# Rounds taken in pairs, and a convolution moved into the weight fold: one change to a fused convolution and feed-forward kernel

## The chip, the core and the metric

The kernel runs on one core of a Trainium2 chip. A core has five engines that run side by side, each with its own queue of instructions in program order: TensorE (PE, matrix products), VectorE (DVE), ScalarE (ACT), GpSimd (POOL) and SyncE (SP). SP and POOL also issue the transfers between the chip's DRAM and the core's SBUF memory. Results of TensorE go to a small memory called PSUM, from which VectorE or ScalarE must copy them away before the place can be used again. The engines meet only at semaphores. The metric is the device time of one launch in microseconds (us), lower is better.

## What is computed

The reference has two stages. First a causal convolution over the sequence (8 sequences of 3904 positions, 192 channels): the channels form 8 heads of 24, each head has 7 taps, and the taps go through a softmax. Then a multiplicative feed-forward layer on all 31232 tokens.

```
w   = softmax(weight, axis=-1)                       # 8 heads x 7 taps
out[b, s, h, g] = sum_k w[h, k] * x_pad[b, s + k, h, g]   # 6 zeros ahead of each sequence
x2  = out.reshape(31232, 192)
a   = x2 @ w1                                        # 192 -> 1024
b   = x2 @ w2                                        # 192 -> 1024
y   = ((a * b) @ w3) @ w_out                         # 1024 -> 1024 -> 192
```

## The kernel before, in words

**Folding.** w3 and w_out are multiplied once (`W_sb` = w3 @ w_out, 1024x192), so that each token needs only two products. The *first product* makes `pa` = x2 @ w1 and `pb` = x2 @ w2, which ScalarE copies (`asb`, L376) and VectorE multiplies (`abT`, L377). The *second product* takes `abT` through `W_sb` (L388), and ScalarE copies the result (`osb`, L393), which SP stores to the output. The *fold of w3* is eight steps: TensorE transposes a row block of w3 (`w3_transpose`, L419), VectorE copies it (`w3T`, L422), TensorE multiplies it with w_out (`w3_product`, L428), ScalarE copies the result into `W_sb` (L430).

**Tiling.** The tokens are split into two streams (`NS` = 2, the first and the last four sequences), held in partitions 0 to 63 and 64 to 127. A *round* R is 512 tokens of each stream. There are 31 rounds, and the last one is half as wide. In a round the first product has eight steps `ft`, each of six matmuls into `pa` and six into `pb`. The second product of a round is two calls, one per stream, of 32 matmuls each.

**The convolution.** It is done on TensorE too. Windows of 64 positions (58 new ones and 6 of overlap) are multiplied with a banded matrix of one head's taps. There are 272 windows per stream, taken in ten *blocks* (`SIZES`). `conv(b, h0, nh)` convolves `nh` heads of block b: four matmuls per head (two halves of the block, two streams), one tile of PSUM (`cps`, L255), and a cast to `convo` (L272) by VectorE or ScalarE. A cast of a head whose 24 channels cross a multiple of 64 is split in two.

**From the convolution to the first product.** Blocks 0 to 2 (10 windows each) are transposed on TensorE (`pe_transposes`, L307) and copied to `xT` (L314). Later blocks are written by SP to a DRAM buffer (`store`, L292 and L298) and read back with transposing transfers (`transposes`, L335) into `xT`, a ring of four rounds.

**PSUM.** There is one pool of four tiles (`banks`, `bufs=4`), each of two banks, for everything: `pa`, `pb`, `ops`, `cps`, the transposes and the fold. They are handed out in turn, so a new tile waits until the tile four places earlier has been copied away.

**Order.** The order of all queues is that of the Python calls (`manual_schedule`). After a start-up (loading, the banded matrices, block 0), the first products of rounds 0, 1 and 2 run with the convolutions of blocks 1, 2 and 3 set between their steps (the `between` argument, L461 and after). Then come the fold, and a loop over R. Each pass of the loop has the first product of R (from R = 3 on), the second product of R - 2, two or three heads of the convolution as `plan` says, a `store` when a block is complete, and the transposing loads that have become possible. `load_x` for a later block is issued on POOL after a small copy (`pace`, L520) that waits for the end of a first product.

Of the kernel before, what the change touches and what calls it, by code (L numbers as in the profile page):

```python
# [17 lines left out]
def kernel(  # L18
# [10 lines left out]
    nc = tc.nc  # L29

    B, S, D = x.shape
    H, K = weight.shape
# [7 lines left out]
    NS = 2  # L40
    TS = B * S // NS
    CH = 512
    NR = -(-TS // CH)
    RING = 4 * CH
    LAG = 2
    Q = 64
    ST = Q - PAD
    NP = D // Q
    WB = -(-S // ST)
    NWIN = (B // NS) * WB  # L50
    LAST = S - (WB - 1) * ST
    SIZES = [10, 10, 10, 30, 32] + [36] * 5
    assert sum(SIZES) == NWIN
    NB = len(SIZES)
    FIRST = [sum(SIZES[:b]) for b in range(NB)]
# [3 lines left out]
    def tok(i):  # L59
        return (i // WB) * S + (i % WB) * ST  # L60
# [11 lines left out]
    def banks_bf16(name):  # L72
        return psum.tile([128, 16, 128], BF16, tag="banks", name=name)
# [18 lines left out]
    def load_x(b, parts=(0, 1)):  # L92
        tiles = xb_of.setdefault(b, [])
        zeros_of = zero_rows.setdefault(b, [])
        for i0, n in [v for e, v in enumerate(halves_of(b)) if e in parts]:
            xb = work.tile([128, n, D], BF16, tag="xb", bufs=6, name="xb")
            w = 0
            if i0 == 0:
                nc.vector.memset(xb[:, 0, :], 0.0)
                for r in range(NS):  # L100
                    nc.gpsimd.dma_start(out=xb[Q * r:Q * r + Q, 1:n, :], in_=x_spans(r, 1, n - 1))  # L101
                w = n
            while w < n:
                i = i0 + w
                m = min(n - w, WB - i % WB)
                at_end = i + m == NWIN
                if at_end:
                    m -= 1
                if m:
                    for r in range(NS):  # L110
                        nc.gpsimd.dma_start(out=xb[Q * r:Q * r + Q, w:w + m, :],  # L111
                                            in_=x_spans(r, i, m))
                if i % WB == 0:
                    zeros_of += [(xb, 0, w), (xb, 1, w)]
                w += m
                if at_end:
                    nc.gpsimd.memset(xb[Q:128, w, :], 0.0)
                    t = tok(NWIN - 1) - PAD
                    nc.gpsimd.dma_start(out=xb[0:Q, w, :], in_=x_rows[t:t + Q, :])
                    nc.gpsimd.dma_start(out=xb[Q:Q + PAD + LAST, w, :],  # L120
                                        in_=x_rows[TS + t:TS + t + PAD + LAST, :])
                    w += 1
            if len(halves_of(b)) == 1:
                tiles += [(xb, 0), (xb, SIZES[b] // 2)]
            else:
                tiles.append((xb, 0))
# [171 lines left out]
                    nc.sync.dma_start(out=dst[s0:s1], in_=src[s0:s1])  # L298
                w += m

    def pe_transposes(b):
        n = SIZES[b] // 2
        convo = convo_of[b]
        tps = banks_bf16("tps")
        for k in range(NP):
            for w in range(n):
                nc.tensor.transpose(  # L307
                    out=tps[:, k * n + w, :],
                    in_=convo[:, w, k].rearrange("p r g -> p (r g)"), identity=ident)
        t0 = tok(FIRST[b])  # L310
        for k in range(NP):
            dst = xT[k][:, t0:t0 + 2 * n * ST].rearrange("p (c w s) -> p c w s", c=2, w=n)
            src = tps[:, k * n:(k + 1) * n, :].rearrange("p w (c s) -> p c w s", c=2)
            (nc.scalar.copy if k == 1 else nc.vector.tensor_copy)(out=dst, in_=src[:, :, :, 0:ST])  # L314

    def pe_transpose(b, k, lead=0):
        n = SIZES[b] // 2
        convo = convo_of[b]
        tps = banks_bf16("tps")
        for w in range(lead):  # L320
            nc.tensor.transpose(out=tps[:, w % 2, :], in_=zeros[:, 0:128], identity=ident)
        for w in range(n):
            nc.tensor.transpose(
                out=tps[:, w, :],
                in_=convo[:, w, k].rearrange("p r g -> p (r g)"), identity=ident)
        t0 = tok(FIRST[b])
        dst = xT[k][:, t0:t0 + 2 * n * ST].rearrange("p (c w s) -> p c w s", c=2, w=n)
        src = tps[:, 0:n, :].rearrange("p w (c s) -> p c w s", c=2)
        return dst, src[:, :, :, 0:ST]

    def transposes(R, first=0):
        t0, t1 = max(R * CH, first), min((R + 1) * CH, TS)
# [21 lines left out]

    def first_product(R, between=None, lead=0):
        N = width(R)
        ab = work.tile([128, JT, NS, CH], BF16, tag="abT", bufs=LAG + 1, name="abT")
        abT_of[R] = ab
        r0 = (R * CH) % RING
        for ft in range(JT):  # L360
            pq = []
            for i in range(2):
                p = banks("pa" if i == 0 else "pb")
                pq.append(p)
                if ft == 0 and i == 0:
                    warm(lead, p)
                for k in range(NP):
                    for r in range(NS):
                        rs = slice(Q * r, Q * r + Q)
                        nc.tensor.matmul(  # L370
                            p[:, r, 0:N], w_of(i, k, r)[rs, ft * 128:(ft + 1) * 128],
                            xT[k][rs, r0:r0 + N],
                            start=(k == 0), stop=(k == NP - 1))
            pa, pb = pq
            asb = work.tile([128, NS, CH], BF16, tag="asb", bufs=3, name="asb")
            nc.scalar.copy(out=asb[:, :, 0:N], in_=pa[:, :, 0:N])  # L376
            nc.vector.tensor_tensor(out=ab[:, ft, :, 0:N], in0=asb[:, :, 0:N],  # L377
                                    in1=pb[:, :, 0:N], op=ALU.mult)
            if between and ft in between:
                between[ft]()  # L380
# [30 lines left out]
    def load_w3(jt):  # L411
        w3b_of[jt] = stage.tile([128, DFF], BF16, tag="w3b", bufs=JT, name="w3b")
        nc.gpsimd.dma_start(out=w3b_of[jt], in_=w3r[:, jt, :])
# [47 lines left out]
    swap_w(1, 0, (V, A))  # L461
    for k in (0, 2, 1):
        swap_w(k, 1, (P, P if k == 1 else V))
    load_x(3)
    load_wo()
    for jt in range(JT):
        load_w3(jt)
    load_x(4)
    load_x(5)

    def seq(*fs):
        def run():
            for f, *a in fs:
                f(*a)
        return run

    first_product(0, lead=2, between={
        3: seq((conv, 1, 0, 4)),
        5: seq((conv, 1, 4, 4)),
        7: seq((pe_transposes, 1), (conv, 2, 0, 4))})  # L480
    first_product(1, {
        0: seq((conv, 2, 4, 4)),
        2: seq((pe_transposes, 2), (store, 2, 26)),
        7: seq((conv, 3, 0, 1), (conv, 3, 1, 1))})
    first_product(2, {
        1: seq((conv, 3, 2, 1), (conv, 3, 3, 1)),
        3: seq((conv, 3, 4, 1), (conv, 3, 5, 1)),
        5: seq((conv, 3, 6, 1), (conv, 3, 7, 1), (store, 3), (transposes, 3), (transposes, 4))})
    sent[0] = 5

    for jt in range(JT):
        w3_transpose(jt)
        if jt > 1:
            w3_product(jt - 2)
    w3_product(JT - 2)
    w3_product(JT - 1)


    plan = {}
    R = LAG  # L500
    for b in range(PROLOGUE_BLOCKS, NB):
        last = tok(FIRST[b]) // CH - (2 if b == PROLOGUE_BLOCKS else 3)
        hs, n = list(range(H)), last - R + 1
        for j in range(n):
            plan[R + j] = [(b, hs.pop(0)) for _ in range(-(-len(hs) // (n - j)))]
        R = last + 1

    pace = const.tile([1, 2], BF16)
    done_of = {}
    for R in range(LAG, NR + LAG):  # L510
        heads = plan.get(R, [])
        if heads:
            b = heads[0][0]
            for xb, r, w in zero_rows.pop(b, []):
                nc.gpsimd.memset(xb[Q * r:Q * r + PAD, w, :], 0.0)
            done_of[b] = done_of.get(b, -1) + 1
        if LAG < R < NR:
            first_product(R)
            if heads and PROLOGUE_BLOCKS < b < NB - 1 and done_of[b] < 2:
                P(out=pace, in_=abT_of[R][0:1, JT - 1, 1, 0:2])  # L520
                load_x(b + 1, (done_of[b],))
        for r in range(NS):
            second_product(R - LAG, r)
        for j, (b, h) in enumerate(heads):
            conv(b, h, 1, (V,) if j < 2 else (A,))
        if heads and heads[-1][1] == H - 1:
            store(b)
        while sent[0] < NR and sent[0] <= R + 3 and min((sent[0] + 1) * CH, TS) <= stored[0]:
            transposes(sent[0])
            sent[0] += 1  # L530


# [28 lines left out]
```

## Time and profile before

| what | value |
|---|---|
| time, median of 3 runs | 539.95 us (539.43 to 540.07) |
| the profiled execution's own time | 540.92 us |
| its span in the profile | 539.1 us |
| TensorE busy (PE) | 527.0 us, 98% |
| VectorE busy (DVE) | 358.1 us, 66% |
| ScalarE busy (ACT) | 317.8 us, 59% |
| GpSimd busy (POOL) | 52.0 us, 10% |
| granted TensorE clock over the span | 0.999 |
| start of the first second product | 66.75 us |
| end of the last second product's copy | 535.5 us |

Busy time is counted per engine. TensorE's matmuls are pipelined and their ends are modelled, so a busy share of 98% hides short waits. These are better read from the start times of groups of matmuls. A round is read from the starts of the three kinds of matmuls in it: `pa`/`pb` (L370), `ops` (L388) and `cps` (L255).

### The profile page before, as it was taken

How to read it: one execution, taken by the hardware profiler on the slowest of the kernel's cores; microseconds unless marked ns; L12 is line 12 of the kernel's file. 1: busy time of each engine (PE TensorE's matmuls, PEld its weight loads, DVE VectorE, ACT ScalarE, POOL GpSimd, SP SyncE). 2: the span in 40 equal slices, each digit the busy share in tenths (PEclk: the TensorE clock that was granted, in tenths of full speed). 3: DMA queues.
4: the chain of work that ended last, by engine and by line, in shares of the span. 5: the costliest groups of instructions: out<-in, count | busy, mean ns of one | idle time of the engine just before them, and what ended most of it. 6: DMA issues, size and time to landing. Idle time of an engine off the chain costs nothing.

```text
span 539.1 us, 12703 instructions
## 1 busy us (share of the span) xinstructions
PE 527.0 (98%) x5469; PEld 343.4 (64%) x5469; DVE 358.1 (66%) x342; ACT 317.8 (59%) x357; POOL 52.0 (10%) x89
## 2 busy tenths in 40 slices
PE   8989999999999999999999999999999999999996
PEld 4443766665666755666656667566665566666586
DVE  6767656678666786666876667866668755557730
ACT  3769455567555566555665555665556655556652
POOL 8733000010101100021000120000000000000000
PEclk9999999999999999999999999999999999999999
DMA  7999961179949893397835978256212653211114
GB/s 91 168 210 192 190 128 60 36 163 179 138 107 153 124 154 89 106 167 105 139 89 134 138 126 128 80 157 140 70 49 60 171 123 89 70 50 46 60 61 148
DMA packets 130541, 63.13 MB, mean 117 GB/s; under 512 B 83352, under 2 KB 129460, under 8 KB 130484
## 3 DMA queue, kind: packets, MB, share of 16 engines
q1 hardware_dynamic: 91764, 45.65, 36.8%
q0 software_dynamic: 38576, 16.63, 26.2%
q8 instruction: 43, 0.70, 0.6%
q14 instruction: 14, 0.11, 0.1%
q10 hardware_dynamic: 144, 0.03, 0.0%
HBM read 33.28 MB, written 34.82 MB: 126 GB/s over the span
## 4 chain that ended last, share of the span: by engine, by line
PE 89%; DVE 3%; ACT 3%; DMA 2%; POOL 2%; issue 1%; ACTq 0%; POOLq 0%
PE ops L388 30%; PE pa L370 28%; PE pb L370 28%; DVE abT L377 2%; PE cps L255 2%; ACT asb L376 2%; DMA xb<-in_x_dram 1%; PE wps L428 1%; DMA xT<-rows 1%; ACT osb L393 1%; PE w3ps L419 0%; POOL cmask L151 0%; POOL xb L101 0%; DVE xT L314 0%; POOL wn L165 0%
## 5 line engine op out<-in xcount | busy, mean ns | idle before, releaser
L377 DVE TENSOR_TENSOR abT<-asb,pb 128x1024 bf16<-128x1024 bf16 (+1 forms) x248 | 298.0, 1204 | 62.9 <-ACT asb L376 49.1
L376 ACT CAST asb<-pa 128x1024 bf16<-128x1024 f32 (+1 forms) x248 | 247.5, 999 | 69.6 <-PE pa L370 68.4
L370 PE MATMUL pb<-xT,wn 64*128 64x512 bf16 (+1 forms) x744 | 201.3, 373 | 0.8 <-DVE abT L377 0.4
L370 PE MATMUL pa<-xT,wn 64*128 64x512 bf16 (+1 forms) x744 | 198.6, 373 | 2.5 <-ACT osb L393 1.0
L370 PE MATMUL pa<-xT,ws 64*128 64x512 bf16 (+1 forms) x744 | 198.6, 373 | 0.3 <-ACT xT L314 0.3
L370 PE MATMUL pb<-xT,ws 64*128 64x512 bf16 (+1 forms) x744 | 194.2, 373 | 0.0
L370 PEld LDWEIGHTS <-wn 64*128 64x128 bf16 x1488 | 136.7, 94 | 87.8 <-issue 10.3
L370 PEld LDWEIGHTS <-ws 64*128 64x128 bf16 x1488 | 128.8, 94 | 72.6 <-issue 7.5
L388 PEld LDWEIGHTS <-abT 128*128 128x128 bf16 x1952 | 159.6, 98 | 11.7 <-issue 11.7
L388 PE MATMUL ops<-W_sb,abT 128*128 128x192 bf16 x1952 | 166.1, 246 | 0.0
L393 ACT COPY osb<-ops 128x768 f32<-128x768 f32 (+1 forms) x62 | 48.8, 788 | 127.6 <-PE ops L388 127.6
L272 DVE CAST convo<-cps 128x864 bf16<-128x864 f32 (+3 forms) x52 | 44.4, 902 | 93.2 <-PE cps L255 89.0
L111 POOL DMA_DIRECT2D xb<-in_x_dram x38 | 29.9, 800 | 8.9 <-DMA w3b<-in_moe_w_dram 3.8
L520 POOL COPY pace<-abT 1x2 bf16<-1x2 bf16 x8 | 1.4, 174 | 250.8 <-DVE abT L377 250.8
L255 PE MATMUL cps<-xb,Aband 64*64 64x432 bf16 (+3 forms) x320 | 18.3, 309 | 1.9 <-DMA xb<-in_x_dram 1.0
L272 ACT CAST convo<-cps 128x720 bf16<-128x720 f32 (+8 forms) x26 | 13.5, 579 | 1.3 <-PE cps L255 1.3
L255 PEld LDWEIGHTS <-Aband 64*64 64x64 bf16 x320 | 6.2, 105 | 10.3 <-issue 8.7
L175 PE MATMUL warm<-zeros 128*128 128x512 bf16 x28 | 8.4, 474 | 1.4 <-DVE wsb L183 1.4
L175 PEld LDWEIGHTS <-zeros 128*128 128x128 bf16 x30 | 3.4, 116 | 6.1 <-issue 3.0
L428 PE MATMUL wps<-wo_b,w3T 128*128 128x192 bf16 x64 | 6.3, 246 | 0.8 <-DVE w3T L422 0.8
L430 ACT CAST W_sb<-wps 128x192 bf16<-128x192 f32 x8 | 2.5, 318 | 7.4 <-PE wps L428 7.4
L422 DVE COPY w3T<-w3ps 128x1024 bf16<-128x1024 bf16 x8 | 5.3, 689 | 1.8 <-PE w3ps L419 1.8
(56 smaller groups left out, 63.4 us busy)
## 6 DMA issues: line engine op xcount, KB each, us to landing
out_dram<-osb SPq DMA_DIRECT2D x60, 384.0 KB
xb<-in_x_dram POOLq DMA_DIRECT2D x14, 432.0 KB, 10.7
rows<-convo SPq DMA_DIRECT2D x7, 648.0 KB
w3b<-in_moe_w_dram POOLq DMA_DIRECT2D x8, 256.0 KB, 12.5
xb<-in_x_dram POOLq DMA_DIRECT2D x6, 240.0 KB, 8.2
xb<-in_x_dram POOLq DMA_DIRECT2D x4, 360.0 KB, 9.3
xT<-rows SPq DMA_TRANSPOSE x84
xb<-in_x_dram POOLq DMA_DIRECT2D x6, 192.0 KB, 9.3
```

What stands on the lines that cost most here:

```text
L111: nc.gpsimd.dma_start(out=xb[Q * r:Q * r + Q, w:w + m, :], in_=x_spans(r, i, m))
L175: nc.tensor.matmul(t[:, j % 2, :], zeros[:, 0:128], zeros, start=True, stop=True)
L255: nc.tensor.matmul(view(slice(Q * c, Q * c + Q), r)[:, :, j * G:(j + 1) * G], band_of(h, r), xb[Q * r:Q * r + Q, w0:w0 + n, h * G:(h + 1) ...
L272: f[e % len(f)](out=dst, in_=part)
L370: nc.tensor.matmul(p[:, r, 0:N], w_of(i, k, r)[rs, ft * 128:(ft + 1) * 128], xT[k][rs, r0:r0 + N], start=(k == 0), stop=(k == NP - 1))
L376: nc.scalar.copy(out=asb[:, :, 0:N], in_=pa[:, :, 0:N])
L377: nc.vector.tensor_tensor(out=ab[:, ft, :, 0:N], in0=asb[:, :, 0:N], in1=pb[:, :, 0:N], op=ALU.mult)
L388: nc.tensor.matmul(ops[:, g // 2, (g % 2) * D:(g % 2) * D + D], ab[:, jt, r, g * 128:(g + 1) * 128], W_sb[:, jt, :], start=(jt == 0), stop ...
L393: nc.scalar.copy(out=osb.rearrange("p (a g) d -> p a (g d)", g=2), in_=ops[:, 0:ng // 2, 0:2 * D])
L422: nc.vector.tensor_copy(out=w3T_of[jt], in_=tps[:, 0:JT, :])
L428: nc.tensor.matmul(wps[:, 0, 0:D], w3T[:, gt, :], wo_b[:, gt, :], start=(gt == 0), stop=(gt == JT - 1))
L430: nc.scalar.copy(out=W_sb[:, jt, :], in_=wps[:, 0, 0:D])
```

## The change

Five things are changed.

1. `SIZES` becomes [10, 10, 10, 32, 36, 36, 36, 36, 36, 30]. Block 3 has 32 windows, and the short block is last.
2. In the first products of rounds 0 to 2, the convolutions of blocks 1 and 2 move to other steps, and block 3 is no longer there. `pe_transposes` takes three tiles of PSUM, one per third of the channels, where it took one. Its three copies go to VectorE, ScalarE and VectorE as before.
3. Block 3 is convolved around the fold of w3: four heads ahead of it (`conv_half(3, 0)`), four after its fifth step (`jt == 4`), then the store and twelve transposing loads (rounds 3 to 6).
4. The loop over rounds becomes a loop over 15 *phases*. A phase has two first products one after the other, then the second product of one round, four heads of the convolution, and the second product of the next round. The casts of the four heads alternate between VectorE and ScalarE, VectorE first. The first phase has no first product, and the last has three second products and no convolution. Twelve phases have heads.
5. The load of w3 and w_out is issued ahead of block 3's input. Block 5's input is loaded in the second phase, no longer in the start-up.

```
-    SIZES = [10, 10, 10, 30, 32] + [36] * 5
+    SIZES = [10, 10, 10, 32] + [36] * 5 + [30]
...
+    def pe_transposes(b):
+        pairs = [pe_transpose(b, k) for k in range(NP)]
+        for f, (dst, src) in zip((nc.vector.tensor_copy, nc.scalar.copy, nc.vector.tensor_copy),
+                                 pairs):
+            f(out=dst, in_=src)
...
-    load_x(3)
     load_wo()
     for jt in range(JT):
         load_w3(jt)
+    load_x(3)
     load_x(4)
-    load_x(5)
...
     first_product(0, lead=2, between={
-        3: seq((conv, 1, 0, 4)),
+        4: seq((conv, 1, 0, 4)),
         5: seq((conv, 1, 4, 4)),
-        7: seq((pe_transposes, 1), (conv, 2, 0, 4))})
+        7: seq((pe_transposes, 1))})
     first_product(1, {
-        0: seq((conv, 2, 4, 4)),
-        2: seq((pe_transposes, 2), (store, 2, 26)),
-        7: seq((conv, 3, 0, 1), (conv, 3, 1, 1))})
-    first_product(2, {
-        1: seq((conv, 3, 2, 1), (conv, 3, 3, 1)),
-        3: seq((conv, 3, 4, 1), (conv, 3, 5, 1)),
-        5: seq((conv, 3, 6, 1), (conv, 3, 7, 1), (store, 3), (transposes, 3), (transposes, 4))})
+        1: seq((conv, 2, 0, 4)),
+        3: seq((conv, 2, 4, 4)),
+        5: seq((pe_transposes, 2), (store, 2, 26))})
+    first_product(2)
+
+    def conv_half(b, e):
+        for j in range(H // 2):
+            conv(b, e * (H // 2) + j, 1, (V,) if j % 2 == 0 else (A,))
+        if e == 1:
+            store(b)
...
+    conv_half(3, 0)
     for jt in range(JT):
         w3_transpose(jt)
         if jt > 1:
             w3_product(jt - 2)
+        if jt == 4:
+            conv_half(3, 1)
+            send(LAG + 4)
...
+    phases = [()] + [(R, R + 1) for R in range(LAG + 1, NR, 2)]
+    for p, rounds in enumerate(phases):
+        b, e = PROLOGUE_BLOCKS + p // 2, p % 2
...
+        for j, R in enumerate(rounds):
             first_product(R)
+            if j == 0 and b + 1 < NB:
                 P(out=pace, in_=abT_of[R][0:1, JT - 1, 1, 0:2])
+                load_x(b + 1, (0, 1) if p == 1 else (e,))
+        last = NR if p == len(phases) - 1 else done + 2
+        for i in range(done, last):
+            for r in range(NS):
+                second_product(i, r)
+            if i == done and b < NB:
+                conv_half(b, e)
+        done = last
+        send(min(NR - 1, LAG + 2 * p + 4))
```

`send(last)` issues the transposing loads of all rounds up to `last` whose tokens have been stored.

More of the change, by code (lines that the diff above doesn't have):

```diff
@@ L299, in store @@
                 w += m
[L301 to L314, printed above, removed]
     def pe_transpose(b, k, lead=0):
@@ L477, with send @@
     first_product(0, lead=2, between={
-        3: seq((conv, 1, 0, 4)),
+        4: seq((conv, 1, 0, 4)),
         5: seq((conv, 1, 4, 4)),
-        7: seq((pe_transposes, 1), (conv, 2, 0, 4))})
+        7: seq((pe_transposes, 1))})
     first_product(1, {
-        0: seq((conv, 2, 4, 4)),
-        2: seq((pe_transposes, 2), (store, 2, 26)),
-        7: seq((conv, 3, 0, 1), (conv, 3, 1, 1))})
-    first_product(2, {
-        1: seq((conv, 3, 2, 1), (conv, 3, 3, 1)),
-        3: seq((conv, 3, 4, 1), (conv, 3, 5, 1)),
-        5: seq((conv, 3, 6, 1), (conv, 3, 7, 1), (store, 3), (transposes, 3), (transposes, 4))})
-    sent[0] = 5
+        1: seq((conv, 2, 0, 4)),
[7 more added lines that the diff above has]
+            store(b)
+    def send(last):
+        while sent[0] <= last and min((sent[0] + 1) * CH, TS) <= stored[0]:
+            transposes(sent[0])
+            sent[0] += 1
+    conv_half(3, 0)
     for jt in range(JT):
@@ L494 @@
             w3_product(jt - 2)
+        if jt == 4:
+            conv_half(3, 1)
+            send(LAG + 4)
     w3_product(JT - 2)
     w3_product(JT - 1)
[L499 to L506, printed above, removed]
-    pace = const.tile([1, 2], BF16)
[L509 to L513, printed above, removed]
+    phases = [()] + [(R, R + 1) for R in range(LAG + 1, NR, 2)]
+    assert phases[-1][-1] == NR - 1
+    pace = const.tile([1, 2], BF16)
+    done = 0
+    for p, rounds in enumerate(phases):
+        b, e = PROLOGUE_BLOCKS + p // 2, p % 2
+        if b < NB:
             for xb, r, w in zero_rows.pop(b, []):
                 nc.gpsimd.memset(xb[Q * r:Q * r + PAD, w, :], 0.0)
-            done_of[b] = done_of.get(b, -1) + 1
-        if LAG < R < NR:
+        for j, R in enumerate(rounds):
             first_product(R)
-            if heads and PROLOGUE_BLOCKS < b < NB - 1 and done_of[b] < 2:
+            if j == 0 and b + 1 < NB:
                 P(out=pace, in_=abT_of[R][0:1, JT - 1, 1, 0:2])
[L521 to L530, printed above, removed]
+                load_x(b + 1, (0, 1) if p == 1 else (e,))
[7 more added lines that the diff above has]
+        send(min(NR - 1, LAG + 2 * p + 4))
+    assert sent[0] == NR
 _INS = ['x', 'weight', 'moe_w1', 'moe_w2', 'moe_w3', 'moe_w_out']
```

## Prediction, made before the changed kernel was run

> **What bounds the kernel now.** I read the page's shares and its chain first, then the list of waits, then the start times of TensorE's groups in one round.
>
> ```profile
> PE 527.0 (98%) x5469; PEld 343.4 (64%) x5469; DVE 358.1 (66%) x342; ACT 317.8 (59%) x357; POOL 52.0 (10%) x89
> ...
> PE 89%; DVE 3%; ACT 3%; DMA 2%; POOL 2%; issue 1%; ACTq 0%; POOLq 0%
> ```
>
> TensorE carries the span, so a gain must be matmul work taken off or a gap in its queue closed. The change takes no matmul away. What gaps are there?
>
> ```profile
> PEld L370 <- DVE convo L272: 1.8, 4, 0.5
> ...
> PE pa L370 <- ACT osb L393: 1.0, 4, 0.3
> ...
> PE pa L370 <- DMA xT<-rows: 0.4, 1, 0.4
> ```
>
> The list puts only some 3 us of gaps on TensorE after the start-up. It hides shorter ones, which the timeline of one round shows (start, duration, instruction):
>
> ```profile
> 249.62 5.45 PE L388 MATMUL ops<-W_sb,abT 128*128 128x192 bf16 x64
> ...
> 255.00 0.56 PE L255 MATMUL cps<-xb,Aband 64*64 64x432 bf16 x8
> 255.10 0.80 ACT L393 COPY osb<-ops 128x768 f32<-128x768 f32 x1 [1.84 <-PE ops L388]
> 255.43 2.09 DVE L272 CAST convo<-cps 128x576 bf16<-128x576 f32 x3 [4.09 <-PE cps L255]
> 255.49 0.39 PE L370 MATMUL pa<-xT,wn 64*128 64x512 bf16 x1
> ...
> 257.57 0.37 PE L370 MATMUL pb<-xT,wn 64*128 64x512 bf16 x1
> ```
>
> A second product takes 5.385 us. Two heads take 0.49, or 0.245 each. One step of a first product is due every 1.295 us (in a round without heads `pa` starts at 436.12, `pb` of step 7 at 445.84, the next `ops` at 446.58). Step 1's `pb` was due at 255.49 + 1.295 + 0.65 = 257.44 and starts at 257.57: its PSUM tile is that of the second head, whose cast ends at 255.43 + 2.09 = 257.52. So a tile four places back is waited for, 0.05 us after its copy ends. The change moves this wait. These durations decide it:
>
> ```profile
> L393 ACT COPY osb<-ops 128x768 f32<-128x768 f32 x60 | 47.9, 798 | 126.2 <-PE ops L388 126.2
> L272 DVE CAST convo<-cps 128x864 bf16<-128x864 f32 x30 | 30.7, 1053 | 61.7 <-PE cps L255 57.6 <-DMA xT<-rows 4.2
> ...
> L272 DVE CAST convo<-cps 128x768 bf16<-128x768 f32 x6 | 5.5, 953 | 15.1 <-PE cps L255 15.1
> ...
> L422 DVE COPY w3T<-w3ps 128x1024 bf16<-128x1024 bf16 x8 | 5.3, 689 | 1.8 <-PE w3ps L419 1.8
> ```
>
> The start-up, up to the first second product at 66.75, from its timeline:
>
> ```profile
> 20.38 0.40 PE L255 MATMUL cps<-xb,Aband 64*64 64x120 bf16 x15 [0.77 <-DMA xb<-in_x_dram]
> ...
> 28.91 0.39 PE L370 MATMUL pa<-xT,wn 64*128 64x512 bf16 x1 [0.80 <-DVE xT L314]
> ...
> 56.84 1.54 PE L419 MATMUL w3ps<-ident,w3b 128*128 128x128 bf16 x24
> 59.23 0.83 PE L428 MATMUL wps<-wo_b,w3T 128*128 128x192 bf16 x8 [0.85 <-DVE w3T L422]
> ```
>
> **The loop, part by part (from 66.75 to the end).**
>
> *Removed, the heads as they stand.* 4 windows of three heads at 0.95 (0.74 of matmuls, the rest the wait for `osb`) and 18 of two at 0.49: 12.6 us.
>
> *Removed, waits inside first products.* Without heads a first product lasts 10.46 us to the next `ops`. Eleven last 10.61 and five 10.54 (the cast above), one 11.03 (0.38 for `xT` from DRAM, and a restart). In all 2.8 us over 27 rounds. After the change the heads are followed by a second product of 5.385 us, which covers casts of c2 and c3 (done 2.7 us after the heads begin). The transposing loads go out a whole phase (over 30 us) ahead, so the wait for `xT` goes too.
>
> *Removed, half the changes from first to second product.* Step 7's `pb` lasts 0.65 and ends at 446.49, `ops` starts at 446.58: 0.09 each. 28 become 14: 1.3 us.
>
> *Added, the window of four heads.* Call its start 0. c0 runs to 0.245, c1 to 0.49, c2 to 0.74. c3 takes the tile of the second `ops`, which ScalarE frees at 0.10 + 0.80, so c3 runs from 0.95 to 1.20. The next `ops` takes c0's tile. VectorE starts that cast 0.43 to 0.51 after the heads begin (0.43 above) and needs 1.05: 0.47 + 1.05 + 0.05 = 1.57. Its second `ops` tile (c1, cast by ScalarE after `osb`, done by 2.0) is due at 4.2: free. Ten windows at 1.57, and two of the short block, whose 720 elements lie between the 576 and 768 rows (0.90 us), at 1.42: 18.5 us. The ends: 0.98 if nothing waits (11.6 in all), and 1.20 if only `osb` does (14.3); above, 2.1 if c2's cast had to end too (25). I take 1.57, since the `pb` at 257.57 shows this very wait. Behind the waiting `ops` stand only its own second product and the next phase, and nobody but TensorE waits for it.
>
> A page of the Trainium skill says otherwise: "Perfetto Trace Analysis", Optimizing Tensor Performance, has independent groups rotate through PSUM banks so that the evacuation of one overlaps the next group's matmuls; by it the window would cost 0.98 and the sum below would be 6.9 us lower. "TensorEngine Tiling (Array Packing)", PSUM Bottleneck, warns the other way, that tiling speeds up TensorE but not the evacuation. The row sides with the second.
>
> *Added, the half round at the end.* Round 30's first product lasts 6.2 us behind a second product (515.38 to 521.56). Now it follows round 29's first product, whose last `abT` ends 1.8 us after its matmuls (448.31 against 446.49). Its first two `pb` wait 0.25 and 0.63 for tiles that VectorE still holds, in place of 0.12 and 0.40 later in it before. VectorE (0.69 us a step against 0.65 of matmuls) doesn't catch up: +0.5, between none and that whole lag of 1.8.
>
> *Even.* VectorE's `abT` runs every 1.286 us over a first product (10.29 for eight), below the 1.295 of TensorE, so sixteen in a row build no backlog. The same stores, loads and output transfers are issued; on SP the output of a phase stands behind at most six transposing loads of 1.3 us (twelve once), with over 20 us to the next use, and five `osb` places last a phase. POOL's `pace` waits for the first of two first products, with `load_x` behind it needed only after 25 us. None of it is on the path.
>
> Loop: 18.5 - 12.6 - 2.8 - 1.3 + 0.5 = +2.3 us.
>
> **The start-up.** *Round 0.* Block 1's heads waited for `xb` until 20.38. One more step (1.295) now fills this. Then VectorE sets the pace: `abT` of step 7 ends near 27.3, the copy to `xT` (0.45) at 27.75, and round 1 starts at 27.8, not 28.91. *Round 1.* 10.36 of products, two sets of heads at 0.33, transposes 0.94, three changes of 0.1, and waits: before about 2.0 (two of them for copies to `xT` that followed one another on one PSUM tile), now I count 0.4 + 0.15 + 0.85 = 1.4 (tiles held by `abT`, then by `xT`). It ends at 41.45 (42.57 before). *Round 2.* 10.36 with no heads: 51.8. Before, it had block 3's six heads, and round 1's end two more, and it ended at 56.74. So 4.9 is gained here.
>
> *The fold.* Count from the end of round 2's matmuls. VectorE ends `abT` at 1.75 (58.48 - 56.74), then casts c0 to 2.70 and the split c2 to 3.68, and copies the first `w3T` (0.63 in a row of three) by 4.31. So the first product of the fold starts at 4.38, where it was 2.5. Three products (0.66) and two transposes (0.445): 7.25. Four heads: 8.18. The next transpose waits for c4's cast (7.68 + 0.95): 8.68, the one after for c7's on ScalarE: 9.78, then 0.445 + 0.66 + 0.445 + 3 x 0.66 = 3.5: 13.3. Before: 10.0. So the fold gives back 3.3. Its ends: 10.8 with no wait, and 15 if the casts and the copies stood in line throughout.
>
> The first second product starts at 51.8 + 13.3 = 65.1: 1.6 us earlier (ends 4.1 earlier and 0.1 later).
>
> *Block 3's way through DRAM.* Its last cast ends at 51.8 + 9.65 = 61.5. Round 3 needs `xT` at 65.1 + 5.39 + 1.57 + 5.39 = 77.4, 15.9 us later. Before, the cast ended at 55.04, the transposing loads began at 62.96 at 1.42 each, so the third was out at 67.2, and no wait showed at 73.08: the way took at most 18.0. With the longest landing in the chain (5.43 for `xT`) it is 17.6, with none 12.2. Ends: 0 and 1.7 us. I take 0, since no input transfers compete now (block 5's moved away).
>
> **Sum.** +2.3 - 1.6 = +0.7 against the profiled execution's 540.92, that is 541.6; this execution was 1.0 above the median. Against the median of 539.95: 540.6. A difference under 0.2% (1.1 us) counts as none.
>
> **Rivals.**
> - *The fold eats the whole gain* (slower). VectorE's casts stand ahead of its `w3T` copies. For: the 0.85 wait at 59.23 was there with no casts at all. Against: the counted queue has TensorE 80% busy. Price: with the start-up at no gain, +2.3, 542.2. It decides once the fold passes 13.7.
> - *Round 3 waits for `xT`* (slower): up to 1.7, 542.3. For: at 123.99 a round waited for such a load, 16 us after the cast. Against: its 0.38 us, with input loads running.
> - *The window is cheaper than read* (faster), the change doing what it looks like: TensorE passes on after `osb` at 1.20, -4.2, 536.4; half of it, 538.5. For: four tiles and two engines casting. Against: the wait at 257.57.
>
> **Chances.** Counted as above, 539.2 to 541.6: 0.52, of it 0.42 within 0.2%, 0.08 slower, 0.02 faster. Fold: 0.18. `xT`: 0.08. Cheaper window or better start-up: 0.22, of it 0.20 faster. The low end of the range is the middle of the cheap window (538.5) less half a microsecond, the high end the slow rivals with as much on top. Faster 0.22, same 0.44, slower 0.34.
>
> **What would show it.** TensorE waits for `convo` casts of VectorE before `ops`, twelve times, each window 1.5 to 1.6 us long; the first `ops` at 65.1 with a fold of 13.3; a pair of first products in 20.8 us without waits; round 3 starting at 77.4. Wrong if a window lasts 1.2 or less, if the first `ops` is before 63.5 or after 66.5, or if `xT` shows as releaser.

## The result

The changed kernel takes 541.18 us (median of 9 runs, 540.57 to 541.99), the kernel before 539.95 (539.43 to 540.46). The ratio is 1.0023 with a 95% interval of 1.0013 to 1.0033: 1.2 us slower, where 0.7 slower was forecast (540.6). The profiled execution of the changed kernel took 540.92, span 539.2: by chance the same as the profiled execution of the kernel before (540.92, span 539.1).

From the page after: the shares of the engines, and the chain that ended last.

```profile
PE 523.8 (97%) x5469; PEld 342.9 (64%) x5469; DVE 343.0 (64%) x325; ACT 331.3 (61%) x374; POOL 51.8 (10%) x90
...
PE 91%; DVE 6%; ACT 2%; DMA 1%; issue 0%; ACTq 0%; DVEq 0%
```

TensorE is busy for 3.2 us less than before (523.8 against 527.0) and the span is no shorter: the rest is gaps. VectorE's share of the chain has doubled from 3% to 6%. TensorE's list of waits after (who waits, for whom; us in all, times, longest) names both gaps of the window:

```profile
PE cps L255 <- ACT osb L384: 2.8, 12, 0.3
PE ops L379 <- DVE convo L272: 2.5, 10, 0.3
...
PE cps L255 <- DVE abT L368: 0.8, 1, 0.8
PE w3ps L410 <- DVE convo L272: 0.6, 1, 0.6
PE wps L419 <- DVE w3T L413: 0.5, 1, 0.5
```

The first window in the timeline after (start, duration, instruction, and in brackets the idle time before it and who ended it):

```profile
70.41 0.74 PE L255 MATMUL cps<-xb,Aband 64*64 64x432 bf16 x12
70.52 0.80 ACT L384 COPY osb<-ops 128x768 f32<-128x768 f32 x1 [1.84 <-PE ops L379]
70.92 1.72 DVE L272 CAST convo<-cps 128x864 bf16<-128x864 f32 x2 [6.97 <-PE cps L255]
...
71.37 0.38 PE L255 MATMUL cps<-xb,Aband 64*64 64x432 bf16 x4 [0.21 <-ACT osb L384]
...
72.03 0.57 PE L379 MATMUL ops<-W_sb,abT 128*128 128x192 bf16 x5 [0.29 <-DVE convo L272]
```

The window runs from 70.41 to 72.03, 1.62 us. The fourth head waits for `osb`. The next `ops` waits for the cast of c0, which began at 70.92, takes 1.06 and ends 0.05 before it. Ten windows are alternately 1.62 and 1.54 long (the cast of c0 begins 0.51 or 0.43 after the heads do), the two of the short block 1.44 and 1.36, 18.59 in all.

The start-up and the fold of w3 after, from TensorE's timeline:

```profile
28.03 0.39 PE L361 MATMUL pa<-xT,wn 64*128 64x512 bf16 x1 [0.95 <-DVE xT L320]
...
51.83 1.00 PE L255 MATMUL cps<-xb,Aband 64*64 64x384 bf16 x12
53.61 0.36 PE L255 MATMUL cps<-xb,Aband 64*64 64x384 bf16 x4 [0.78 <-DVE abT L368]
...
56.00 0.83 PE L419 MATMUL wps<-wo_b,w3T 128*128 128x192 bf16 x8 [0.48 <-DVE w3T L413]
...
60.40 0.61 PE L410 MATMUL w3ps<-ident,w3b 128*128 128x128 bf16 x8 [0.57 <-DVE convo L272]
...
65.04 0.74 PE L379 MATMUL ops<-W_sb,abT 128*128 128x192 bf16 x7
```

Round 2 ends at 51.83, the fold takes 13.2, the first second product starts at 65.04 and round 3 at 77.40 without a wait.

### The profile page after: what moved, and what is told of

Same layout as the page of the kernel before. It is cut to its first block, busy times and chain, and to the rows that moved or that the text cites. A ratio compares the mean times of both kernels' runs of the same rounds, so it can differ in the third digit from the quotient of the medians.

```text
span 539.2 us, 12715 instructions
## 1 busy us (share of the span) xinstructions
PE 523.8 (97%) x5469; PEld 342.9 (64%) x5469; DVE 343.0 (64%) x325; ACT 331.3 (61%) x374; POOL 51.8 (10%) x90
## 4 chain that ended last, share of the span: by engine, by line
PE 91%; DVE 6%; ACT 2%; DMA 1%; issue 0%; ACTq 0%; DVEq 0%
PE ops L379 31%; PE pa L361 29%; PE pb L361 28%; DVE convo L272 3%; DVE abT L368 1%; ACT asb L367 1%; PE wps L419 1%; PE cps L255 1%; DMA wall<-in_weight_dram 1%; PE w3ps L410 0%; DVE cprod L214 0%; PE tps L308 0%; DVE cprod L207 0%; DVE convo L429 0%; DVE Aband L217 0%
## 5 line engine op out<-in xcount | busy, mean ns | idle before, releaser
L361 PEld LDWEIGHTS <-ws 64*128 64x128 bf16 x1488 | 130.2, 94 | 72.9 <-issue 2.1
L272 DVE CAST convo<-cps 128x864 bf16<-128x864 f32 (+8 forms) x35 | 27.7, 842 | 52.5 <-PE cps L255 52.5
L272 ACT CAST convo<-cps 128x864 bf16<-128x864 f32 (+10 forms) x43 | 27.2, 695 | 1.1 <-PE cps L255 0.9
L255 PEld LDWEIGHTS <-Aband 64*64 64x64 bf16 x320 | 8.3, 105 | 13.3 <-issue 11.2
```

The source lines that it names most:

```text
L255: nc.tensor.matmul(view(slice(Q * c, Q * c + Q), r)[:, :, j * G:(j + 1) * G], band_of(h, r), xb[Q * r:Q * r + Q, w0:w0 + n, h * G:(h + 1) ...
L272: f[e % len(f)](out=dst, in_=part)
L361: nc.tensor.matmul(p[:, r, 0:N], w_of(i, k, r)[rs, ft * 128:(ft + 1) * 128], xT[k][rs, r0:r0 + N], start=(k == 0), stop=(k == NP - 1))
```

## Experiments

Every kernel below computes the whole reference. "Loop" means the time from the first `ops` (matmul of a second product) to the start of the last group of them, in one profiled execution. Ratios are to the kernel before, run beside it on the same chip.

**1. The kernel before, once more.** No edit.

> The kernel before, unchanged, once more, for a second profile and for spans of many executions. The two profiled executions took 540.92 us each, yet the medians are 539.95 and 541.18. Theory A: the start-up of the first profile of before was a slow draw (its wait for block 1's input until 20.38 us changes from execution to execution), so here the first second product starts 0.5 to 1.2 us before 66.75, and the rest, from there to the end of the last matmul, takes 468.3 us within 0.3. Theory B: the loop varies instead: the first second product is at 66.75 within 0.3 and the loop is about 1 us shorter.

Measured 539.64 us, ratio 0.9994 (0.998 to 1.0008); the profiled execution took 539.40, span 537.7. Two lines of its timeline:

```profile
19.49 0.40 PE L255 MATMUL cps<-xb,Aband 64*64 64x120 bf16 x16
...
28.04 0.39 PE L370 MATMUL pa<-xT,wn 64*128 64x512 bf16 x1 [0.80 <-DVE xT L314]
```

Block 1's heads start at 19.49 without a wait, where the first profile waited for `xb` until 20.38, and round 1 starts at 28.04, just where it does after the change (28.03). The first `ops` is at 65.88 (66.75 in the first profile), and the loop takes 454.24 (454.81; the 0.57 between them is the one round that waited for `xT` at 123.99). So the profile that the prediction was worked out from was a late draw of the input, 1.5 us above this one, and both of its late transfers lay in steps that the change moves. Against this second profile the change gains 0.84 in the start-up, not 1.7, and loses 2.37 in the loop.

**2. The new start-up with the old loop.** New block sizes, start-up and fold; rounds one by one as before.

```
-    phases = [()] + [(R, R + 1) for R in range(LAG + 1, NR, 2)]
...
+    for R in range(LAG, NR + LAG):
+        heads = plan.get(R, [])
...
+    load_x(5)
```

> The start-up of the changed kernel (block 3 around the fold, transposes in three tiles, blocks of its sizes) in front of the loop as it was before: single rounds, two heads or three after each second product. Theory A (gain of the start-up 1.6 us, as predicted): first second product near 65.1 us, the loop costs the same as before within 0.5, 538.3 to 539 us. Rival: the start-up's gain is only that of one slow profile of before: 539.5 to 540.5 us.

Measured 545.86 us, nine executions from 541.24 to 547.37 and one of 552.89, ratio 1.0081 (1.0051 to 1.0111). The first `ops` is at 65.05, as in the changed kernel, and the gain is lost at once. TensorE in round 3:

```profile
72.29 0.39 PE L361 MATMUL pa<-xT,wn 64*128 64x512 bf16 x1 [1.31 <-DMA xT<-rows]
73.32 0.37 PE L361 MATMUL pa<-xT,ws 64*128 64x512 bf16 x1 [0.64 <-DMA xT<-rows]
74.77 0.37 PE L361 MATMUL pa<-xT,wn 64*128 64x512 bf16 x1 [1.05 <-DMA xT<-rows]
```

Without pairs only one second product stands between the fold and round 3, which is due at 70.98, and the last third of block 3's `xT` is there at 74.77 (the expectations of runs 7 and 9 put it at 75.8, which was misread). The changed kernel's round 3 comes at 77.40, 2.6 us behind that. In these kernels the early fold pays only together with the pairs. A later round, begun at 140.52, waited 2.5 us for `xT` and lasted 14.98 in place of 10.47: the mean granted clock over it was 0.89.

**3. The new loop with the old start-up and block sizes.**

```
-    SIZES = [10, 10, 10, 32] + [36] * 5 + [30]
+    SIZES = [10, 10, 10, 30, 32] + [36] * 5
...
-            if j == 0 and b + 1 < NB:
+            if j == 0 and p > 1 and b + 1 < NB:
```

> The start-up as it was before, with the loop in pairs of rounds and four heads between the second products of a pair. Theory (each window of four heads costs 1.57 us because the next second product waits for the first head's cast): windows of 1.5 to 1.6 us, pairs of first products at 20.83 us, +1.9 to +2.3 us against before: 541.8 to 542.3 us. Rival, that the windows cost no more than the heads' matmuls (0.98): -4 us or more.

Measured 556.81 us, ratio 1.0305 (1.0281 to 1.0328). The windows are those of the changed kernel (1.50 and 1.42, then 1.62 and 1.54), but with the old sizes a pair's second round needs rows that are stored only a phase earlier. From its list of waits:

```profile
PE pa L370 <- DMA xT<-rows: 9.8, 13, 1.9
PE cps L255 <- ACT osb L393: 2.7, 12, 0.3
PE ops L388 <- DVE convo L272: 2.6, 11, 0.3
```

The waits for `xT` lengthen every second pair of first products from 20.83 us to between 21.9 and 24.7. The count of windows points to the block sizes as the reason: the old ones store 60 windows (3480 tokens, six full rounds) ahead of the loop, the new ones 62 (3596, seven). The run left out the new start-up as well, so the sizes were not tested by themselves. Runs 2 and 3 show that its two halves don't add up: each alone is slower than both together.

**4. One head behind each half of a second product.**

```
-            if i == done and b < NB:
-                conv_half(b, e)
+                if i - done < 2 and b < NB:
+                    conv(b, e * (H // 2) + 2 * (i - done) + r, 1, (A,) if r == 0 else (V,))
```

> The changed kernel with one edit: the four heads of a phase stand one behind each of the four halves of its two second products, cast by ScalarE, VectorE, ScalarE, VectorE, so that every PSUM tile has a half (2.7 us) or more to be copied away. Theory (the wait for the first head's cast is the whole excess of the window): each head costs 0.245 us, four 0.98 instead of 1.57 (0.86 instead of 1.40 for the short block): 10 x 0.59 + 2 x 0.54 = 7.0 us less than the changed kernel, 534.2 us, first products without a wait. Rival, that changes between the kinds of matmul cost time themselves: eight more changes in each of twelve phases at 0.09 us would take 6 to 8 us back, 540 us or more.

Measured 539.62 us, ratio 0.9989 (0.9979 to 0.9999); loop 455.26 against 456.61. Both waits of the window are gone from the list, and yet only 1.35 us are gained in the loop. One phase of TensorE's timeline shows what took their place:

```profile
197.21 2.81 PE L379 MATMUL ops<-W_sb,abT 128*128 128x192 bf16 x32
199.95 0.38 PE L255 MATMUL cps<-xb,Aband 64*64 64x432 bf16 x4
200.26 2.81 PE L379 MATMUL ops<-W_sb,abT 128*128 128x192 bf16 x32
```

A head alone costs 0.31 from start to start, where one in a row of two costs 0.245, and a half that stands by itself takes 2.74, where it takes 2.69 in an uncut second product. Over the loop the heads are down by 4.00 us (14.59 against 18.59), and the second products, in 50 runs in place of 26, up by 2.64: 0.11 for each further run.

**5. Two heads between the halves of each second product.**

```
             for r in range(NS):
                 second_product(i, r)
+                if r == 0 and i - done < 2 and b < NB:
+                    for j, f in enumerate((V, A)):
+                        conv(b, e * (H // 2) + 2 * (i - done) + j, 1, (f,))
-            if i == done and b < NB:
-                conv_half(b, e)
```

> Edit to the changed kernel: two heads between the two halves of each of the two second products of a phase, cast by VectorE and ScalarE. No tile of the ring is then waited for: the next ops takes the tile of the half before the heads, copied out 0.5 us and more earlier. Measured so far: the changed kernel spends 12.33 us from the first ops of a phase to the next first product (window 1.62 or 1.54, four halves of 2.69), the version with single heads 12.21 (0.308 for a head alone, 2.745 for a half cut off). Theory of the waits alone (a head is 0.245 wherever it stands): 4 x 0.245 + 4 x 2.69 = 11.74 a phase, -0.59 x 12 = -7.1 us, about 534 us. Theory of a price per change between heads and second product (0.12 for a group, 0.055 for each half cut off): 2 x 0.49 + 4 x 2.745 = 11.96, -0.37 x 12 = -4.4 us, about 536.7 us. Null (casts or copies turn up as a new wait in the first products): 539 to 541 us.

Measured 535.41 us (535.34 to 535.5), ratio 0.9916 (0.9903 to 0.9928): 5.8 us below the changed kernel and faster than both. From TensorE's timeline:

```profile
195.76 2.81 PE L379 MATMUL ops<-W_sb,abT 128*128 128x192 bf16 x32
198.51 0.56 PE L255 MATMUL cps<-xb,Aband 64*64 64x432 bf16 x8
199.00 5.45 PE L379 MATMUL ops<-W_sb,abT 128*128 128x192 bf16 x64
204.38 0.56 PE L255 MATMUL cps<-xb,Aband 64*64 64x432 bf16 x8
204.88 2.81 PE L379 MATMUL ops<-W_sb,abT 128*128 128x192 bf16 x32
```

Each pair of heads takes 0.49 and nothing waits. A phase has three runs of second products in place of two and costs 11.85 where it cost 12.33. The result lies between the two theories. The second products cost 1.43 more over the loop, 0.12 for each of the 12 runs of matmuls that are added: the price of a cut goes by these, one a phase, and not by every half.

**6. Two heads behind each second product.** As in run 5, with the heads behind the loop over `r`.

> Edit to the changed kernel: two heads after the first second product of a phase and two after the second, cast by VectorE and ScalarE. Second products are not cut. The second pair of heads stands directly ahead of a first product, whose step 1 takes its two tiles: one step's pb waited 0.13 for such a tile in the kernel before. Theory of the waits alone: 2 x 0.49 + 0.13 = 1.11 in place of 1.58 a phase, -0.47 x 12 = -5.6 us, about 535.5 us. Theory of a price per change: the same two groups at 0.49, and no half cut off, so the same -5.6 us; it differs from the waits in what it says of the run with the heads amid the second products, which should then be 1.2 us slower than this one, where the waits alone have it 1.5 us faster. Null: a wait for the second pair's casts longer than 0.5 us a phase, 541 us.

Measured 536.12 us, ratio 0.9929 (0.9916 to 0.9941): 0.7 slower than run 5. Second products stay whole, but ten of the twelve pairs of first products, which now follow two heads directly, take 21.01 us in place of 20.83. Over the loop the first products cost 2.04 more than in run 5 and the second products 1.29 less. One pair in the timeline:

```profile
208.12 0.89 ACT L272 CAST convo<-cps 128x864 bf16<-128x864 f32 x1
...
208.89 2.09 ACT L367 CAST asb<-pa 128x1024 bf16<-128x1024 f32 x2
...
209.96 2.35 DVE L368 TENSOR_TENSOR abT<-asb,pb 128x1024 bf16<-128x1024 bf16 x2 [1.08 <-PE pa L361]
...
211.23 0.37 PE L361 MATMUL pb<-xT,wn 64*128 64x512 bf16 x1
```

This is not the wait that was expected, of step 1's `pb` for a head's cast: that `pb` starts 1.95 after the pair's first `pa`, as in run 5. The 0.17 is lost at step 2's `pb` (3.42 after the start, 3.25 in run 5). It needs the tile of step 0's `pb`, which VectorE frees with the first `abT` at 209.96 + 1.22 = 211.18. That `abT` is late because the first `asb` stands behind the second head's cast on ScalarE: it begins 1.08 after the pair's start, and 0.87 in run 5.

**7. Other casts in the fold.**

```
-            conv(b, e * (H // 2) + j, 1, (V,) if j % 2 == 0 else (A,))
+            conv(b, e * (H // 2) + j, 1, ((A, V, A, A) if b == 3 else (V, A, V, A))[j:j + 1])
```

> Edit to the changed kernel: in the two groups of four heads of block 3 in the fold of w3, VectorE casts the second head alone and ScalarE the other three (before: two each, VectorE first). The fold takes 13.2 us, of it 10.8 matmul work. Theory (VectorE's queue of abT, casts and w3T copies ends the waits of the fold): the first w3T copy ends at 55.15 in place of 55.9, so the first wps starts about 0.8 us earlier, and the 0.57 wait after the second group falls to 0.3 or 0.4: first second product at about 64.0 in place of 65.04, -1.0 us, 540.2 us. But round 3 then starts at 76.4, and xT of block 3 lands at about 75.8, so this margin may be used up: a wait of up to 0.5. Rival (the fold is set by TensorE's own work and by abT of round 2): no change, 541.2 us.

Measured 539.88 us, ratio 1.0002 (0.9994 to 1.0011): 1.3 below the changed kernel. TensorE in the fold:

```profile
53.17 0.36 PE L255 MATMUL cps<-xb,Aband 64*64 64x384 bf16 x4 [0.33 <-ACT convo L272]
...
55.09 0.83 PE L419 MATMUL wps<-wo_b,w3T 128*128 128x192 bf16 x8
...
59.32 0.61 PE L410 MATMUL w3ps<-ident,w3b 128*128 128x128 bf16 x8 [0.41 <-ACT convo L272]
...
63.96 0.74 PE L379 MATMUL ops<-W_sb,abT 128*128 128x192 bf16 x7
```

The first `wps` starts 0.91 earlier and no longer waits, and the first `ops` 1.08 earlier; round 3 starts at 76.32 without a wait. VectorE's queue of `abT`, casts and copies did end the waits of the fold.

**8. Block 1's heads one step earlier.**

```
-        4: seq((conv, 1, 0, 4)),
+        3: seq((conv, 1, 0, 4)),
```

> Edit to the changed kernel: block 1's first four heads again in step 3 of round 0, as in the kernel before, and not in step 4. As my prediction had it, this would bring back a wait for xb and round 1 would start at 28.9: +1.1 us, 542.3 us. By the second profile of the kernel before, in which xb had landed in time and round 1 started at 28.04, the step was worth nothing but in executions whose input is late: round 1 at 28.0, no change (541.2 us) with at most a wider spread upwards.

Measured 541.19 us, ratio 1.0025 (1.0016 to 1.0035): the same as the changed kernel. The heads start at 19.47 in its profile, with no wait, and round 1 at 28.02. Moving the step is worth nothing when the input is there. The heads of step 3 waited for `xb` in two of the five profiles that have them there (the first one and run 11), and those of step 4 in none of eight. That is too few to say how often the input is late.

**9. Runs 5 and 7 together.**

> Both edits together: two heads amid each of the two second products of a phase (by itself 535.41 us), and the casts of block 3 in the fold as second head on VectorE, the others on ScalarE (by itself -1.3 us in the median, first second product at 63.96 in place of 65.04). Theory (the two are in series on TensorE): 535.41 - 1.1 = 534.3 us, round 3 at 63.96 + 11.85 = 75.81. Rival: xT of block 3 is late. Its transposing loads began at 67.48 in the run with the fold's casts (67.81 without), and in the run with the start-up alone the last third had landed only at about 75.8, so a wait of 0 to 0.5 appears before round 3, and 534.3 to 534.8 us.

Measured 534.36 us (533.84 to 534.36), ratio 0.9895 (0.988 to 0.991): the fastest kernel here, 6.8 us below the changed one. Round 3 starts at 75.36 with no wait for `xT`, and no wait of the loop is left in the list. It was expected at 75.81; in this profile round 0 already starts 0.44 earlier than in run 7's (12.88 against 13.32).

**10. The engines change places in the window.** In the changed kernel, VectorE copies the `ops` ahead of the window, and ScalarE casts c0 and c2.

```
-                second_product(i, r)
+                second_product(i, r, V if i == done and r == 1 and b < NB else A)
...
-            conv(b, e * (H // 2) + j, 1, (V,) if j % 2 == 0 else (A,))
+            conv(b, e * (H // 2) + j, 1, (V,) if (j % 2 == 0) == (b == 3) else (A,))
```

> Edit to the changed kernel: the two engines change places in the window. VectorE copies the second ops of the first second product to osb, ScalarE casts heads c0 and c2, VectorE c1 and c3. ScalarE then begins c0's cast at 0.45 and needs 0.84, where VectorE needs 1.05. My prediction's mechanism (the next ops takes c0's tile and starts 0.05 after its cast): window 0.45 + 0.84 + 0.05 = 1.35 in place of 1.62, if VectorE's copy of osb takes no more than 0.95 (then c3 runs 1.0 to 1.25): -0.2 to -0.3 x 10 windows = -2 to -2.7 us, 538.5 to 539.2 us, and the waits of ops for convo show ScalarE or nothing. Rival (the window is set by osb's place or by the change of matmul kind, not by the cast): no change, 541.2 us, or +0.1 x 12 if VectorE's copy of osb takes 0.1 longer than ScalarE's.

Measured 539.56 us, ratio 0.9991 (0.9982 to 0.9999): 1.6 below the changed kernel, loop 455.25 against 456.61. The first window:

```profile
70.41 0.74 PE L255 MATMUL cps<-xb,Aband 64*64 64x432 bf16 x12
70.52 0.96 DVE L384 COPY osb<-ops 128x768 f32<-128x768 f32 x1 [6.57 <-PE ops L379]
70.92 1.72 ACT L272 CAST convo<-cps 128x864 bf16<-128x864 f32 x3 [2.24 <-PE cps L255]
...
71.53 0.38 PE L255 MATMUL cps<-xb,Aband 64*64 64x432 bf16 x4 [0.38 <-DVE osb L384]
...
71.85 1.57 PE L379 MATMUL ops<-W_sb,abT 128*128 128x192 bf16 x17
```

The wait of `ops` for a cast is gone from the list, and the windows take 1.44 and 1.43 in turn. The faster cast shortens the window, so it was the cast that held it. The gain is below the one expected because VectorE's copy of `osb` takes 0.96, where ScalarE's takes 0.80: the fourth head starts 1.12 after the first, not 1.0, and with the 0.31 of a head alone (run 4) that gives 1.43. In the windows of 1.43 the cast of c0 ends at 1.31, so `osb` ends them; in those of 1.44 it ends at 1.39, and the two paths are too close to tell apart.

**11. The kernel before, with its heads between the halves.** Rounds one by one.

```
             second_product(R - LAG, r)
-        for j, (b, h) in enumerate(heads):
-            conv(b, h, 1, (V,) if j < 2 else (A,))
+            if r == 0:
+                for j, (b, h) in enumerate(heads):
+                    conv(b, h, 1, (V,) if j < 2 else (A,))
```

> Edit to the kernel before: the two or three heads of a round stand between the two halves of its second product, rounds one by one as before. It asks how much of the gain of the version with two heads amid a second product is due to their place and how much to the pairs. Theory (both count): the waits in the first products go (eleven times 0.15 and five times 0.08, 2.05 us), the four windows of three heads stay at about 0.95 (the second half now waits for the copy of the first), and each of 22 second products gets 0.055 longer by the cut (1.2 us): -0.9 us, 539 us; the changes from first to second product (28 x 0.09, half of them gone in pairs) and the second 0.055 remain. Rival (the place alone is the whole gain): -4.5 us, about 535.3 us. Against: the heads' place is worse there than behind the second product: over 540.2 us.

Measured 540.62 us, ratio 1.0017 (1.0 to 1.0034): no gain. Every first product now takes 10.47 us (10.54 to 10.62 before, with heads), which saves 2.05, and 22 second products cut in two cost 2.28 more, 0.104 each. In its profile, too, block 1's heads waited for `xb`, until 20.68. The expectation charged half a cut, 0.055, for each second product; a cut costs 0.1. So the place of the heads by itself gains nothing here. The loop of run 5 is 3.46 us shorter than this one: 1.21 of it is in the second products (38 runs in place of 50), 1.17 in first products taken in pairs, and 1.08 in the heads (no window of three, which still waits for `osb` here and takes 0.96).

## Why the prediction was right, and which terms were not

The loop's own groups, from TensorE's start times (us; the kernel before by its second profile, run 1):

| | before | after | run 5 |
|---|---|---|---|
| heads | 12.64 | 18.59 | 11.56 |
| first products | 290.85 | 287.63 | 287.63 |
| second products | 150.75 | 150.40 | 151.82 |
| loop | 454.24 | 456.61 | 451.01 |

- *The window of four heads.* Predicted 1.57 each and 18.5 in all, measured 1.62 and 1.54, 18.59. The mechanism is shown by the wait for `convo` (ten times; the short block's two are not in the list) and by run 10, where a shorter cast shortens the window. The `pb` at 257.57 of the kernel before was the right row to read: a tile four places back is free only when its cast ends. The Trainium skill, "Perfetto Trace Analysis", Optimizing Tensor Performance, advises that independent groups rotate through PSUM banks, so that the evacuation of one overlaps the next group's matmuls. With such an overlap the window would have taken an estimated 0.98 (four heads at 0.245). The four heads in a row did not get it; the two pairs of run 5 did (0.49 each), where at least half a second product lies between a tile and its next use.
- *Heads as they stood, 12.6.* Measured 12.64.
- *First products: -2.8 for waits, -1.3 for changes, +0.5 for the last half round, -3.6 together.* Measured -3.79 against the first profile and -3.22 against the second, which has no wait for `xT`. The waits of the first profile come to 2.65, not 2.8: twelve rounds lasted 10.61, where eleven were counted, and even with twelve the listed terms stay below 2.8. The last half round follows round 29 with 16.86 us for both, against 10.47 + 6.18 before. The change saved there, 0.1, is already in the 1.3, so the half round cost +0.3, not +0.5.
- *Second products: even.* Measured -0.36 in all: a small term that was not counted.
- *The loop, +2.3.* +2.37 against the second profile, +1.80 against the first.
- *The start-up, step by step.* Round 1 at 27.8 (28.03), the end of round 2 at 51.8 (51.83), the fold 13.3 (13.2), the first `ops` at 65.1 (65.04), round 3 at 77.4 with `xT` in time (77.40, no wait). Run 7 shows that the counted cause, VectorE's queue, was right too.
- *The start-up's gain, -1.6: the term that was mis-sized.* Against the profile that it was worked out from it is -1.71. Against the second profile it is -0.84. The step that failed was to take the wait for `xb` until 20.38 as something that the kernel before always pays, and then also to take that execution's 1.0 us above the median off the sum: the late input was in the gain and in the offset at once. The 0.57 for `xT` in the loop was counted in the same way. With the second profile's values the sum is +2.37 - 0.84 = +1.5; the medians differ by 1.2.
- *How near the number came is in part luck.* Against the first profile the two parts measured +1.80 and -1.71, +0.1 in all, so the sum of +0.7 was 0.6 too slow. That made up for half of the error of the offset, which was on the other side: the first profile lay 1.0 above its kernel's median, the changed kernel's profile 0.3 below its own. The 1.2 us measured lie just over the 0.2% (1.1 us) that the prediction counts as no difference, with an interval on both sides of it: slower, to which it gave 0.34, rather than same (0.44).
- *The rivals.* The fold did not eat the gain (13.2, below 13.7). `xT` was not late, but run 2 shows that it would have been without the pairs. The cheaper window did not come by itself: both of its waits went away when the heads were moved (runs 4 to 6), and one of them, for the cast, when the engines changed places (run 10).

## What to carry to other kernels

Before work is gathered into one longer group, count the buffers of the ring it runs through: the group waits as soon as its next tile is one whose copy began in the same group, and two smaller groups with other matmuls between them then beat one large one (0.49 + 0.49 against 1.62 here). Weigh that against the cost of one more cut, about 0.1 us here, and look for a place where one cut serves two neighbours. When a profiled execution lies above the median, look for the late transfers that put it there: if the change moves just those steps, their wait must not be counted as a gain and be taken off with the offset again.

## What the runs showed that was not expected

- Cutting a second product's row of matmuls with 64x64 heads costs about 0.11 us for each further run of them (2.64 us over 24 in run 4, 2.28 over 22 in run 11, 1.43 over 12 in run 5), with no wait in the trace. A head alone takes 0.31, where two take 0.49. The Trainium skill, "TensorEngine Tiling (Array Packing)", Key Properties, says that a change of tiling mode drains TensorE. The runs agree with that in sign and place, and give it a size here; that the drain is the cause was not tested by itself.
- The input of block 1 was in time in one profile of the unchanged start-up (19.49) and late in another (20.38), which moved the whole start-up by 0.87 us.
- An early first `ops` can be worse than a late one: in run 2 it brought round 3 forward to 70.98, where it waited 3.0 us in three steps for `xT`, and a later round waited 2.5 more and lasted 4.5 longer, with a granted clock of 0.89.
